# Attention rows stacked as high and low halves per head, W made already stacked, and row tiles of 64 for both products with W

## The chip, the cores and the metric

The kernel runs on one core of one Trainium2 chip. The metric is the device time in microseconds of one execution, the median of three.

## What is computed

Eight batches of eight heads, 576 positions, head dimension 64. First an attention with 32 landmarks per head (Nyström), then a mixing of positions and channels by Fourier transforms, then a feed-forward layer:

```python
q_lm = q.reshape(B, H, 32, 18, 64).mean(axis=3)      # and k_lm
A, Bm, C = sm(q, k_lm), sm(q_lm, k_lm), sm(q_lm, k)  # softmax of scaled scores
Z = Bm.T / (norm1(Bm) * norminf(Bm) + 1e-6)
for _ in range(6):
    Z = 2 * Z - Z @ Bm @ Z
x = A @ Z @ C @ v                                    # heads side by side: 576 x 512
u = x + real(fft(fft(x, axis=positions), axis=channels))
un = (u - mean(u)) / sqrt(var(u) + 1e-6)
out = u + maximum(un @ w_ch1, 0) @ w_ch2             # 512 -> 2048 -> 512
```

## The kernel before, in words

Numbers are held to more than half precision as two fp16 parts, high and low; a product of two such numbers is three matmuls (high by high, high by low, low by high), written `mm3`. W stands for Z C v, 32 x 64 per head.

**Order of work.** The program first records all operations with their reads and writes (`Order.op`), and then a planner (`Order.solve`) places them engine by engine by phase and rank, with estimated durations (`cost_of`, `mm`), buffers and PSUM banks being handed out as it goes. Operations between `together` and `apart` become one bundle on TensorE. Each engine then runs its list in that order. Attention of all batches has the higher priority, the feed-forward chunks fill in. Of the PSUM banks four are "at" (attention), two "hp", two "acc"; from chunk 5 on, two of the "at" banks are kept by the feed-forward part (`seven`, `held_banks`). SBUF buffers called "mt" (512 columns, five of them) are handed out in the order of their making.

**A batch** (`attention`): landmarks by reduction, the splits of q, and then `landmarks`, which makes the softmax of B (`nrm`), the scores of C, and six iterations on `RE`, whose columns 0 to 31 are the iterated matrix and 32 to 95 become the factor of W; a head is a block of 32 partitions, four blocks for each of two groups g of four heads. W = `RE` part times `nrm`, in two orientations: `ps` (landmarks on partitions) and `pst` (channels on partitions). After the scale `sc` (a sum over W, `pow2`), twelve splits (each a ScalarE operation and a VectorE one) move W into two kept tiles that are zero elsewhere: `Wx`, block diagonal for four heads with 256 columns, and `Wt`, two heads stacked in 128 rows.

**A's rows.** The scores of A are taken for three tiles u (two of 512 columns, a rest of 128), the softmax goes to `ae`, which is split into `hl` as all high parts and then all low parts, and transposed by DMA into `AT` (y for high and low, then four blocks of 128).

**The two products with W.** `rest()` multiplies `Wt` with the cosine and sine tables `t2`: four bundles (g, x) of six matmuls, 128 rows by 64 columns of weights, 262 moving columns, the two results in halves of one bank. `mix` runs over three row tiles nt: first the sums of CS with those results, then for each sign sg a bundle of six matmuls, `AT` as weights and `Wx` moving with 256 columns, then three additions on VectorE into the row tile `u`, which goes on to `norm` and the feed-forward chunks.

**Feed-forward.** `chunk` and, from chunk 5 on, `seven` take two row tiles (256 rows) each through `w1` and `w2`, whose preparation (`weights`, `sums_of`, `differences_of`) lies in the first part of the program.

All operations are issued through one helper, so the profile gives them all the line L1184; they are told apart by tile names: `at`, `hp`, `acc` are PSUM banks, `t` the tables.

Of the kernel before, what the change touches and what calls it, by code (L numbers as in the profile page):

```python
# [60 lines left out]
def tables():  # L61
# [8 lines left out]
    for x, fn in enumerate((np.cos, np.sin)):  # L70
        t1t[:, x] = trig(fn, REST * 2, freqs[0::2] + freqs[1::2], S)
        for r in range(4):
            h0, h1 = GROUPS[r // 2][2 * (r % 2) : 2 * (r % 2) + 2]
            cols = [*range(D * h0, D * h0 + D), *range(D * h1 + D - 1, D * h1 - 1, -1)]
            t2[:, r, :, x] = trig(fn, cols, [f or 0 for f in FREQS], DM) * np.array(there)
# [30 lines left out]
class View:  # L106
# [42 lines left out]
    def box(self):  # L149
# [5 lines left out]
        high = low + sum(step * (n - 1) for step, n in ap[1:]) + 1  # L155
# [215 lines left out]
def cost_of(engine):  # L371
# [3 lines left out]
    def cost(name, out, reads, rest):  # L375
# [19 lines left out]
class Kernel:  # L395
    def __init__(self, ctx, tc, NB, q, k, v, w1, w2, t1, t1t, t2, diag, mask, out):
# [230 lines left out]
    def attention(self, b):  # L627
# [61 lines left out]
        for u in range(3):  # L689
# [25 lines left out]
        for u in range(3):  # L715
            ae, w = aes[u], 512 if u < 2 else 128
            AT = (self.mid(512).bitcast(F16) if u < 2 else self.small(256, "AT2", F16)).rearrange("p (y t) -> p y t", y=2)
            hl = (self.row(1024, F16) if u < 2 else self.small(256, "hl2", F16)).rearrange("p (y t) -> p y t", y=2)
            self.A.copy(hl[:, 0], ae)
            self.E.tensor_tensor(hl[:, 1], ae, hl[:, 0], ALU.subtract)  # L720
            for y in range(2):
                self.turn(AT[:, y].rearrange("p (c t) -> p c t", t=P), hl[:, y])
            ATs.append(AT)
            if u == 2:
                Fs.append(hl)
                break
# [34 lines left out]
    def landmarks(self, b, loads, qbd, lm):  # L761
# [70 lines left out]
        V.tensor_scalar(nci, ci, -1.0, None, ALU.mult)  # L832
        BT = small([P, 2, 32], "BT", bufs=1)
# [62 lines left out]
        wm = small(1, "wm")  # L896
        V.tensor_reduce(wm, ps[:, 0:128], AX.X, ALU.add, apply_absolute_value=True)
        ew, rw = self.pow2(wm, 1, "wx")
# [5 lines left out]
        for o in range(2):  # L904
            rows = slice(64 * o, 64 * o + 64)
            for r in range(2):
                self.split(
                    *(Wt[rows, y, r::2, 32 * o : 32 * o + 32] for y in range(2)),
                    pst[r][rows, 0:64].rearrange("p (g m) -> p g m", g=2), sc[rows, 0:1],
                )  # L910
        for i, at in enumerate((0, 32, 160, 128)):
            rows = slice(32 * i, 32 * i + 32)
            wv = Wx[rows, :, :, at : at + 96]
            pv = ps[rows, 0:128].rearrange("p (g m o) -> p g m o", g=2, o=2)
            for o in range(2):
                self.split(*(wv[:, y, :, 64 * o : 64 * o + 32] for y in range(2)), pv[..., o if i % 2 == 0 else 1 - o], sc[rows, 0:1])

        def rest():
            WC = [self.mid().bitcast(F16)[:, 0 : 4 * NC].rearrange("p (y x t) -> p y x t", y=2, x=2) for g in range(2)]
            for g in range(2):  # L920
                for x in range(2):
                    ps = self.at()
                    self.order.claim(WC[g])
                    self.together()
                    for ya, yb in ((0, 0), (0, 1), (1, 0)):
                        for r in range(2):
                            mm(ps[64 * r : 64 * r + 64, 0:NC], Wt[:, ya, 2 * g + r, :], self.t2[:, 2 * g + r, yb, x, :],
                               yb == 0 and ya == 0, ya == 1, 0.5)
                    self.apart()
                    self.split(WC[g][:, 0, x], WC[g][:, 1, x], ps[:, 0:NC], 2.0**-15)  # L930
# [4 lines left out]
    def mix(self, b, AT, CS, WC, Wx, x2, x13):  # L935
# [3 lines left out]
        for nt in range(3):  # L939
# [18 lines left out]
            uts = []  # L958
            for sg in range(2 if nt < 2 else 1):
                ps = self.at()  # L960
                at = P * (3 - nt if sg else nt)
                pv = ps.rearrange("p (a m) -> p a m", a=8)
                if nt < 2:
                    ut = self.new("u")
                elif b2 == 0:
# [286 lines left out]
```

## Time and profile before

| | us |
|---|---|
| median of 3 runs | 1012.71 |
| lowest and highest | 1012.39, 1014.78 |
| the profiled execution | 1016.18 |
| its span, first to last instruction | 1014.40 |
| its TensorE clock, mean | 0.976 of full speed |

The profile is of one execution. The groups of instructions name what is written and read; `PE` is the matmul stream, `PEld` the loading of weights, which overlaps it. A matmul's own duration includes its way through the array, so it is the distance of two starts that says what one costs. Most rows of interest are therefore from the timeline: the start of the group that follows, less the start of this one.

### The profile page before, as it was taken

Reading aid. Unit: us, or ns where it says so; the run is one execution under the profiler, and the core shown is the slowest. Engines: PE = TensorE matmul, PEld = TensorE weight load, DVE = VectorE, ACT = ScalarE, POOL = GpSimd, SP = SyncE. Lnnn points to the kernel's source line nnn. Section 1 sums busy time; section 2 is a strip of 40 time slices with the busy share of each in tenths; the row PEclk is TensorE's granted clock in tenths of the full one; section 3 lists DMA queues with packets and bytes.
Section 4 is the critical chain, followed back from the end, with each engine's and each line's share of the span. In section 5 each row is a group of like instructions: output and inputs, shape, how many; then the busy total and the mean of one; then the engine's idle time right before and its main releaser. Section 6 shows DMA issues by size and latency. Waiting matters only on the chain.

```text
span 1014.4 us, 24771 instructions
## 1 busy us (share of the span) xinstructions
PE 948.1 (93%) x9858; PEld 751.9 (74%) x9858; DVE 778.6 (77%) x2082; ACT 488.6 (48%) x1045; POOL 191.3 (19%) x218
## 2 busy tenths in 40 slices
PE   4566998999999999999999999999999999999997
PEld 3345656666667567888888888888888788888886
DVE  6989896699897898668986888698976657575455
ACT  5989843245543443445553655355533343433332
POOL 0211020024542122122112033122211110011010
PEclk9697998999999999999999999999999999999999
DMA  9965010444422312345434533443343413344231
GB/s 342 314 252 160 24 35 12 128 117 96 175 85 62 98 54 45 89 116 173 123 94 122 168 89 104 131 150 122 104 115 90 120 48 95 94 118 126 87 100 47
DMA packets 139396, 117.28 MB, mean 116 GB/s; under 512 B 66704, under 2 KB 128144, under 8 KB 139152
## 3 DMA queue, kind: packets, MB, share of 16 engines
q1 hardware_dynamic: 139280, 115.69, 38.2%
q8 instruction: 77, 1.26, 0.5%
q14 instruction: 39, 0.32, 0.1%
HBM read 88.91 MB, written 12.58 MB: 100 GB/s over the span
## 4 chain that ended last, share of the span: by engine, by line
PE 66%; DVE 17%; ACT 9%; DMA 3%; issue 2%; SPq 1%; POOL 0%; DVEq 0%; ACTq 0%
PE hp L1184 29%; PE at L1184 20%; PE acc L1184 18%; DVE u L1184 2%; ACT w L1184 2%; ACT Wx L1184 2%; DVE Wx L1184 1%; DVE mt L1184 1%; DVE ws L1184 1%; DVE h L1184 1%; ACT ws L1184 1%; DVE row L1184 1%; DMA big<-k_dram 1%; ACT big L1184 1%; DVE lm L1184 1%
## 5 line engine op out<-in xcount | busy, mean ns | idle before, releaser
L1184 PEld LDWEIGHTS <-w 128*128 128x128 f16 (+1 forms) x3584 | 344.8, 99 | 66.5 <-DVE w L1184 12.9
L1184 PE MATMUL hp<-unT,w 128*128 128x256 f16 x3264 | 390.5, 275 | 0.1
L1184 PEld LDWEIGHTS <-h 128*128 128x128 f16 x2508 | 239.0, 98 | 66.8 <-issue 5.8
L1184 PE MATMUL acc<-w,h 128*128 128x256 f16 (+1 forms) x1260 | 205.3, 300 | 0.4 <-DVE h L1184 0.2
L1184 DVE TENSOR_TENSOR sum<-ws 128x256 f32<-128x256 f32 (+1 forms) x261 | 94.9, 410 | 96.3 <-ACT ws L1184 92.7
L1184 ACT ACTIVATE ws<-hp 128x512 f32<-128x512 f32 x104 | 62.0, 596 | 165.4 <-PE hp L1184 165.2
L1184 ACT CAST h<-sum 128x640 f16<-128x640 f32 x104 | 75.4, 725 | 64.8 <-DVE sum L1184 50.9
L1184 PE MATMUL at<-big,h 128*128 128x256 f16 x624 | 102.2, 273 | 0.0
L1184 POOL TENSOR_TENSOR sum<-ws 128x256 f32<-128x256 f32 (+1 forms) x51 | 36.2, 723 | 307.6 <-ACT ws L1184 224.6
L1184 DVE TENSOR_TENSOR h<-sum,h 128x640 f16<-128x640 f32 x83 | 68.4, 824 | 24.3 <-ACT h L1184 23.8
L1184 DVE TENSOR_REDUCE lm<-big 128x32 f32<-128x576 f32 (+1 forms) x48 | 44.7, 945 | 17.9 <-DMA big<-k_dram 16.0
L1184 PE MATMUL at<-w,h 128*128 128x256 f16 x312 | 51.1, 273 | 0.0
L1184 PE MATMUL acc<-big,h 128*128 128x256 f16 x312 | 51.1, 273 | 0.0
L1184 PEld LDWEIGHTS <-mt 128*128 128x128 f16 x432 | 39.5, 102 | 14.8 <-issue 5.7
L1184 PEld LDWEIGHTS <-big 128*128 128x128 f16 (+1 forms) x768 | 39.6, 103 | 10.5 <-issue 5.6
L1184 ACT CAST h<-ws 128x256 f16<-128x256 f32 x104 | 42.1, 405 | 2.8
L1184 DVE SCALAR_TENSOR_TENSOR u<-at,scw,row 128x128 f32<-128x128 f32 (+3 forms) x120 | 39.6, 387 | 2.6 <-PE at L1184 2.2
L1184 DVE SCALAR_TENSOR_TENSOR u<-acc,winv,u 128x512 f32<-128x512 f32 x49 | 34.8, 745 | 7.1 <-PE acc L1184 7.1
L1184 POOL TENSOR_TENSOR h<-sum,h 128x640 f16<-128x640 f32 x21 | 30.9, 1470 | 47.7 <-ACT h L1184 47.7
L1184 DVE TENSOR_TENSOR h<-ws,h 128x256 f16<-128x256 f32 x87 | 36.3, 418 | 0.0
L1184 POOL TENSOR_TENSOR ws<-ws 128x256 f32<-128x256 f32 (+1 forms) x31 | 24.2, 788 | 52.2 <-DVE ws L1184 26.3
L1184 ACT ACTIVATE big<-big 128x1168 f16<-128x1168 f32 (+1 forms) x26 | 25.4, 990 | 14.9 <-DMA big<-q_dram 14.5
(192 smaller groups left out, 1362.9 us busy)
## 6 DMA issues: line engine op xcount, KB each, us to landing
big<-sums SPq DMA_DIRECT2D x312, 128.0 KB, 2.1
w<-w_dram SPq DMA_DIRECT2D x22, 512.0 KB, 7.9
big<-v_dram SPq DMA_DIRECT2D x16, 640.0 KB, 4.7
big<-q_dram SPq DMA_DIRECT2D x16, 584.0 KB, 5.8
big<-k_dram SPq DMA_DIRECT2D x16, 576.0 KB, 5.3
out_dram<-u SPq DMA_DIRECT2D x36, 256.0 KB, 2.3
big<-w_dram SPq DMA_DIRECT2D x10, 512.0 KB, 5.4
sums<-ws SPq DMA_DIRECT2D x24, 128.0 KB, 1.7
```

The source lines that it names most:

```text
L1184: getattr(engine, name)(*map(real, args), **{k: real(x) for k, x in kw.items()})
```

## The change

Four things are done. (1) A's softmax is written as head, then high and low, then 32 landmarks, so that a transposed block holds two heads, each with its high and low part in 64 rows; the rest tile keeps its plain split in `rest` and gets one more copy. (2) W comes from products with block-diagonal copies of `nrm` (`nbd`, two elementwise operations of 256 columns), which hold the landmarks twice, so that each head's W leaves TensorE twice, one copy below the other, for the high and the low rows of A: two fp32 matmuls for `pst` and eight for `ps`, over 128 rows; two wide splits take the place of twelve, and nothing has to be zeroed. (3) Both products with W use halves of 64 rows; the product with `t2` has two bundles of 24 matmuls (tiles of 64 rows by 32 columns, a bank for each g), the mix one bundle for both signs, two matmuls of 64 columns for each head (high and low part of `Wx`; the weights hold both parts of A, so low by low is included), a bank for each half of the rows. (4) The planner's estimates are changed for small operations, and edges are added between uses of the banks. The tables `t2` change their layout with it, and the extent of a view with a negative step is computed.

The diff, with the tables and the extent of views left out:

```diff
-            return 0.07 + rate * n + 0.03 * pointers, 0.08, not psum and (full > 1 or quick) and n > 4
+            least = 0.28 if psum and pointers and out.dtype == F16 else 0.0
+            return max(least, 0.07 + rate * n + 0.055 * pointers), 0.08, not psum and (full > 1 or quick) and n > 4
...
-            return 0.09 + 0.79e-3 * n + (0.06 if pointers else 0.0) + extra, 0.1, False
+            least = 0.31 if psum and pointers and out.dtype == F16 else 0.0
+            return max(least, 0.09 + 0.79e-3 * n + (0.08 if pointers else 0.0)) + extra, 0.1, False
...
-        self.Wx = self.kept([P, 2, 2, 256], F16, "Wx")
-        self.Wt = self.kept([P, 2, 4, 64], F16, "Wt")
-        for t in (self.Wx, self.Wt):
-            self.G.memset(t, 0.0)
+        self.Wx = self.kept([P, 2, 4, 64], F16, "Wx")
+        self.Wt = self.kept([P, 2, 4, 32], F16, "Wt")
...
-            held = max(0.03, 0.003 + n / 2400 * share)
+            held = max(0.02, 0.003 + n / 2400 * share + (0.01 if share < 1.0 or 100 < n < 200 else 0.0))
...
-                    mm3(ps[rows, at + 64 * pr : at + 64 * pr + 64],
+                    mm3(ps[rows, at : at + 128].rearrange("p (h r m) -> p h r m", h=2, r=2)[:, :, pr],
...
-            hl = (self.row(1024, F16) if u < 2 else self.small(256, "hl2", F16)).rearrange("p (y t) -> p y t", y=2)
-            self.A.copy(hl[:, 0], ae)
-            self.E.tensor_tensor(hl[:, 1], ae, hl[:, 0], ALU.subtract)
-            for y in range(2):
-                self.turn(AT[:, y].rearrange("p (c t) -> p c t", t=P), hl[:, y])
+            hl = self.row(1024, F16) if u < 2 else self.small(256, "hl2", F16)
+            hy = hl.rearrange("p (h y m) -> p h y m", y=2, m=32)
+            av = ae.rearrange("p (h m) -> p h m", m=32)
+            if u == 2:
+                rest = self.small([P, 2, 128], "rest", F16, bufs=1)
+                self.A.copy(rest[:, 0], ae)
+                self.E.tensor_tensor(rest[:, 1], ae, rest[:, 0], ALU.subtract)
+                self.A.copy(hy, rest.rearrange("p y (h m) -> p h y m", m=32))
+            else:
+                self.A.copy(hy[:, :, 0], av)
+                self.E.tensor_tensor(hy[:, :, 1], av, hy[:, :, 0], ALU.subtract)
+            for x in range(0, 8 if u < 2 else 2, 4):
+                n = min(4, AT.shape[1])
+                self.turn(AT[:, x : x + n], hl[:, P * x : P * x + P * n])
...
+        nbd = self.mid(512).rearrange("p (g i m) -> p g i m", g=2, i=4)
+        for g in range(2):
+            self.E.tensor_tensor(
+                nbd[:, g].rearrange("p i (d m) -> p i d m", d=2), nrm[:, g, 0].unsqueeze(1).unsqueeze(1).broadcast_to([P, 4, 2, 32]),
+                self.mask4.unsqueeze(2).unsqueeze(3).broadcast_to([P, 4, 2, 32]), ALU.mult,
+            )
...
-        ps, pst = self.at(), [self.at(), self.at()]
+        pst = self.at()
         self.together()
         for g in range(2):
-            for i in blocks:
-                mm(ps[i, 64 * g : 64 * g + 64], nrm[i, g, 0, :], RE[i, g, 32:])
+            mm(pst[64 * g : 64 * g + 64, 0:128], RE[:, g, 32:], nbd[:, g, :, 0:32])
         self.apart()
+        self.order.ops[-1].before.update(self.used[1])
+        self.used[1] = {}
+        wm = small(1, "wm")
+        V.tensor_reduce(wm, pst[:, 0:128], AX.X, ALU.add, apply_absolute_value=True)
+        count = len(self.order.ops)
+        ew, rw = self.pow2(wm, 1, "wx")
+        total = self.order.ops[count]
+        ps = self.at()
         self.together()
         for g in range(2):
-            for i, rows in enumerate(blocks):
-                o, r = i % 2, i // 2
-                mm(pst[r][64 * o : 64 * o + 64, 32 * g : 32 * g + 32], RE[rows, g, 32:], nrm[rows, g, 0, :])
+            for i in range(4):
+                at = 64 * (2 * g + i % 2)
+                w = RE[:, g, 32:].rearrange("p (m o) -> p o m", o=2)
+                mm(ps[64 * (i // 2) : 64 * (i // 2) + 64, at : at + 64], nbd[:, g, i],
+                   w[:, ::-1] if i % 2 else w)
         self.apart()
...
+        self.order.ops[-1].before[total] = None
+        self.order.ops[-1].before.update(self.used[0])
+        self.used[0] = {}
...
-        for o in range(2):
-            rows = slice(64 * o, 64 * o + 64)
-            for r in range(2):
-                self.split(
...
-        for i, at in enumerate((0, 32, 160, 128)):
...
-            for o in range(2):
-                self.split(*(wv[:, y, :, 64 * o : 64 * o + 32] for y in range(2)), pv[..., o if i % 2 == 0 else 1 - o], sc[rows, 0:1])
+        for W, src in ((Wt, pst[:, 0:128]), (Wx, ps[:, 0:256])):
+            self.split(*(W[:, y].rearrange("p a b -> p (a b)") for y in range(2)), src, sc[:, 0:1])
...
-            for g in range(2):
-                for x in range(2):
-                    ps = self.at()
...
-                    for ya, yb in ((0, 0), (0, 1), (1, 0)):
-                        for r in range(2):
-                            mm(ps[64 * r : 64 * r + 64, 0:NC], Wt[:, ya, 2 * g + r, :], self.t2[:, 2 * g + r, yb, x, :],
...
+            for x in range(2):
+                pss = [self.at(), self.at()]
...
+                for ya, yb in ((0, 0), (0, 1), (1, 0)):
+                    for i in range(4):
+                        at = 32 * (2 * (i % 2) + i // 2)
+                        for g in range(2):
+                            rows = slice(64 * g, 64 * g + 64)
+                            mm(pss[g][at : at + 32, 0:NC], Wt[rows, ya, i], self.t2[rows, i, yb, x], yb == 0 and ya == 0, ya == 1, 0.125)
+                self.apart()
+                self.used[1][self.order.ops[-1]] = None
...
-            for sg in range(2 if nt < 2 else 1):
-                ps = self.at()
...
-                for g in range(2):
-                    mm3(pv[rows, :, 32 * g : 32 * g + 32], lambda y: AT[g][:, y, at : at + P] if nt < 2 else AT[2][:, y, 64 * g : 64 * g + 64],
-                        lambda y: Wx[:, y, g, :])
...
+            banks = [self.at(), self.at()]
+            self.order.claim(*uts)
+            self.together()
+            for sg in range(count):
+                for g in range(2):
+                    for pair in range(2):
+                        for y in range(2):
+                            for e in range(2):
+                                half = slice(64 * e, 64 * e + 64)
+                                at = 256 * sg + 64 * (pair if e == 0 else 1 - pair) + 32 * g
+                                to = banks[e][rows].rearrange("p (a m) -> p a m", m=32)[:, at // 32 : at // 32 + 5 : 4]
+                                lhs = AT[g][half, 2 * (3 - nt if sg else nt) + pair] if nt < 2 else AT[2][half, pair, 64 * g : 64 * g + 64]
+                                mm(to, lhs, Wx[half, y, 2 * g + pair], y == 0, y == 1, 0.5)
+            self.apart()
+            self.order.ops[-1].before[sums] = None
+            self.used[0][self.order.ops[-1]] = None
```

## Rows read from the trace of the kernel before

**Rows 1.** The page, busy time (us), share of the span and instructions of each engine.

```profile
PE 948.1 (93%) x9858; PEld 751.9 (74%) x9858; DVE 778.6 (77%) x2082; ACT 488.6 (48%) x1045; POOL 191.3 (19%) x218
```

**Rows 2.** The busy time of each engine by stretch: the stretch in us and its length, then for each engine busy us and (x instructions), then the granted clock of TensorE as a share of full speed, the busy share of the DMA engines and GB/s.

```profile
25.00:100.00 75.00, 44.89 (x509) 34.36 (x507) 68.36 (x180) 69.59 (x145) 14.23 (x13) 0.78 0.76 240
100.00:400.00 300.00, 288.56 (x3016) 193.56 (x3014) 253.09 (x690) 140.30 (x336) 72.96 (x80) 0.99 0.28 79
400.00:900.00 500.00, 494.04 (x5196) 419.24 (x5195) 381.65 (x1019) 226.24 (x470) 94.69 (x108) 1.00 0.38 113
```

**Rows 3.** TensorE's timeline around one pair of row tiles of the product with Wx: start us, us from the first start to the last end (matmuls overlap), engine, line, operation, out<-in with the active rows*columns, shape of the moving operand, count.

```profile
502.83 1.47 PE L1184 MATMUL at<-Wx,mt 128*128 128x256 f16 x12
504.14 0.49 PE L1184 MATMUL acc<-w,h 128*128 128x256 f16 x3
```

**Rows 4.** The same view around the last row tile of 64 rows.

```profile
838.53 0.49 PE L1184 MATMUL at<-big,h 128*128 128x256 f16 x3
838.95 0.84 PE L1184 MATMUL at<-Wx,AT 128*64 128x256 f16 x6
839.72 0.50 PE L1184 MATMUL at<-w,h 128*128 128x256 f16 x3
```

**Rows 5.** The same view around half of the product of Wt with the tables.

```profile
682.99 0.49 PE L1184 MATMUL acc<-w,h 128*128 128x256 f16 x3
683.41 0.86 PE L1184 MATMUL at<-t,Wt 128*64 128x262 f16 x12
684.21 0.50 PE L1184 MATMUL acc<-w,h 128*128 128x256 f16 x3
```

**Rows 6.** The same view around the sums of the rest tile (operands hl and t1t, 64 rows in each half), from the end of the sums of 160 columns on.

```profile
470.03 0.51 PE L1184 MATMUL at<-t,mt 128*128 128x160 f16 x5
470.47 0.58 PE L1184 MATMUL at<-t1t,hl 64*128 64x320 f16 x6
470.98 0.39 PE L1184 MATMUL hp<-unT,w 128*128 128x256 f16 x2
```

**Rows 7.** The same view around matmuls of 64 columns with weights of 128*128 (the scores of A).

```profile
517.47 0.86 PE L1184 MATMUL at<-kbd,big 128*128 128x64 f16 x24
518.16 0.41 PE L1184 MATMUL at<-ident,ml 128*128 128x128 f32 x2
```

**Rows 8.** The same view around the two products that make W.

```profile
252.84 0.81 PE L1184 MATMUL acc<-w,sum 128*128 128x512 f16 x3
253.58 0.43 PE L1184 MATMUL at<-RE,nrm 32*32 32x64 f32 x16
253.94 0.43 PE L1184 MATMUL at<-nrm,RE 32*64 32x32 f32 x16
254.31 0.39 PE L1184 MATMUL hp<-big,w 128*128 128x256 f16 x2
```

**Rows 9.** The same view around the fp32 products of 288 columns in two column tiles (scores of C).

```profile
107.02 1.19 PE L1184 MATMUL at<-big,qbd 128*64 128x288 f32 x8
108.04 0.37 PE L1184 MATMUL at<-lm,qbd 128*64 128x32 f32 x8
```

**Rows 10.** What TensorE waited for from 100 us on: us in total, times, the longest.

```profile
PE at L1184 <- DVE Wx L1184: 8.2, 6, 2.2
...
PE at L1184 <- ACT Wx L1184: 0.7, 1, 0.7
...
PE at L1184 <- DVE Wt L1184: 0.2, 1, 0.2
```

**Rows 11.** Groups of instructions, shapes kept apart: out<-in, shapes, count, then busy us and mean ns of one, then the idle time before them and who ended it. First ScalarE, then VectorE.

```profile
L1184 ACT CAST h<-ws 128x256 f16<-128x256 f32 x104 | 42.1, 405 | 2.8
...
L1184 ACT ACTIVATE Wx<-at,scw 32x64 f16<-32x64 f32 x64 | 19.6, 306 | 13.9 <-DVE Wx L1184 9.6 <-PE at L1184 3.3 <-DVE scw L1184 0.5
...
L1184 ACT ACTIVATE Wt<-at,scw 64x64 f16<-64x64 f32 x32 | 9.9, 309 | 10.9 <-PE at L1184 7.4 <-DVE scw L1184 2.9
...
L1184 ACT ACTIVATE row<-at,scw 128x262 f32<-128x262 f32 x16 | 7.8, 486 | 10.1 <-PE at L1184 10.1
...
L1184 DVE TENSOR_TENSOR mt<-mt 128x256 f32<-128x256 f32 x44 | 22.7, 534 | 2.1 <-PE at L1184 1.2 <-POOL mt L1184 0.8
...
L1184 DVE SCALAR_TENSOR_TENSOR u<-at,scw,row 128x128 f32<-128x128 f32 x64 | 18.8, 341 | 0.0
...
L1184 DVE SCALAR_TENSOR_TENSOR Wx<-at,scw,Wx 32x64 f16<-32x64 f32 x64 | 17.9, 280 | 8.0 <-ACT Wx L1184 7.0
...
L1184 DVE SCALAR_TENSOR_TENSOR row<-at,scw,row 128x262 f32<-128x262 f32 x32 | 14.2, 481 | 5.3 <-ACT row L1184 5.3
...
L1184 DVE SCALAR_TENSOR_TENSOR Wt<-at,scw,Wt 64x64 f16<-64x64 f32 x32 | 9.0, 282 | 1.9 <-ACT Wt L1184 1.3
```

**Rows 12.** The timeline of all engines from 805.2 to 808.5 us, the splits of the last batch's W and the matmul that waits for one of their banks.

```profile
805.21 0.30 ACT L1184 ACTIVATE Wx<-at,scw 32x64 f16<-32x64 f32 x1 [0.63 <-DVE Wx L1184]
...
805.55 0.28 DVE L1184 SCALAR_TENSOR_TENSOR Wx<-at,scw,Wx 32x64 f16<-32x64 f32 x1 [0.37 <-ACT Wx L1184]
805.86 0.31 ACT L1184 ACTIVATE Wx<-at,scw 32x64 f16<-32x64 f32 x1 [0.35 <-DVE Wx L1184]
...
805.93 0.30 PE L1184 MATMUL at<-nrm,RE 32*64 32x32 f32 x4
...
808.45 0.42 PE L1184 MATMUL at<-nrm,RE 32*64 32x32 f32 x12 [2.21 <-DVE Wx L1184]
```

More of the change, by code (lines that the diff above doesn't have):

```diff
@@ L71, in tables @@
         t1t[:, x] = trig(fn, REST * 2, freqs[0::2] + freqs[1::2], S)
[L72 to L75, printed above, removed]
+        for g in range(2):
+            for i, h in enumerate(GROUPS[g]):
+                cols = [*range(D * h, D * h + D)][:: -1 if i % 2 else 1]
+                t2[64 * g : 64 * g + 64, i, :, x] = trig(fn, cols, [f or 0 for f in FREQS], DM) * np.array(there)
     p = np.arange(P)
@@ L154, in box @@
         low = self.ap.offset - first * ap[0][0]
-        high = low + sum(step * (n - 1) for step, n in ap[1:]) + 1
+        high = low + sum(max(0, step) * (n - 1) for step, n in ap[1:]) + 1
+        low += sum(min(0, step) * (n - 1) for step, n in ap[1:])
         return first, first + ap[0][1], low * size, high * size
@@ L918, in rest @@
         def rest():
             WC = [self.mid().bitcast(F16)[:, 0 : 4 * NC].rearrange("p (y x t) -> p y x t", y=2, x=2) for g in range(2)]
-            for g in range(2):
-                for x in range(2):
-                    ps = self.at()
-                    self.order.claim(WC[g])
-                    self.together()
-                    for ya, yb in ((0, 0), (0, 1), (1, 0)):
-                        for r in range(2):
-                            mm(ps[64 * r : 64 * r + 64, 0:NC], Wt[:, ya, 2 * g + r, :], self.t2[:, 2 * g + r, yb, x, :],
-                               yb == 0 and ya == 0, ya == 1, 0.5)
-                    self.apart()
-                    self.split(WC[g][:, 0, x], WC[g][:, 1, x], ps[:, 0:NC], 2.0**-15)
+            for x in range(2):
+                pss = [self.at(), self.at()]
+                self.order.claim(*WC)
+                self.together()
[7 more added lines that the diff above has]
+                self.used[1][self.order.ops[-1]] = None
+                for g in range(2):
+                    self.split(WC[g][:, 0, x], WC[g][:, 1, x], pss[g][:, 0:NC], 2.0**-15)
@@ L957, in mix @@
                 V.scalar_tensor_tensor(Tt[rows, x, 0:NC], psc[rows, 0:NC], x2[rows], Qs[rows], ALU.mult, op)
-            uts = []
-            for sg in range(2 if nt < 2 else 1):
-                ps = self.at()
[L961 to L965, printed above, removed]
-                    ut = self.uR = self.new("u")
-                else:
-                    ut = self.uR
-                self.order.claim(ut)
-                self.together()
-                for g in range(2):
-                    mm3(pv[rows, :, 32 * g : 32 * g + 32], lambda y: AT[g][:, y, at : at + P] if nt < 2 else AT[2][:, y, 64 * g : 64 * g + 64],
-                        lambda y: Wx[:, y, g, :])
-                self.apart()
-                self.order.ops[-1].before[sums] = None
-                uts.append(ut)
+            count = 2 if nt < 2 else 1
@@ new lines, in mix @@
+            uts = [self.uR] if nt == 2 and b2 else [self.new("u") for sg in range(count)]
+            if nt == 2:
+                self.uR = uts[0]
+            banks = [self.at(), self.at()]
+            self.order.claim(*uts)
+            self.together()
+            for sg in range(count):
+                for g in range(2):
+                    for pair in range(2):
[6 more added lines that the diff above has]
+                                mm(to, lhs, Wx[half, y, 2 * g + pair], y == 0, y == 1, 0.5)
@@ L977, in mix @@
+            self.apart()
+            self.order.ops[-1].before[sums] = None
+            self.used[0][self.order.ops[-1]] = None
+            for sg, ut in enumerate(uts):
                 t0, t1 = Tt[rows, sg], Tt[rows, 1 - sg]
                 runs = lambda t: t.rearrange("p (x m) -> p x m", x=4)[:, :, 0:64]
-                u4, p4 = (t[rows].rearrange("p (x m) -> p x m", x=8) for t in (ut, ps))
-                V.scalar_tensor_tensor(u4[:, 0:4], p4[:, 0:4], x13[rows], runs(t0), ALU.mult, ALU.add)
+                u4 = ut[rows].rearrange("p (x m) -> p x m", x=8)
+                p4 = [t[rows, 256 * sg : 256 * sg + 256].rearrange("p (x m) -> p x m", x=4) for t in banks]
+                V.scalar_tensor_tensor(u4[:, 0:4], p4[0], x13[rows], runs(t0), ALU.mult, ALU.add)
@@ L981, in mix @@
                 V.scalar_tensor_tensor(
-                    u4[:, 4:6], p4[:, 4:6], x13[rows], t1[:, 1:129].rearrange("p (x m) -> p x m", x=2), ALU.mult, ALU.add
+                    u4[:, 4:6], p4[1][:, 0:2], x13[rows], t1[:, 1:129].rearrange("p (x m) -> p x m", x=2), ALU.mult, ALU.add
                 )
-                V.scalar_tensor_tensor(u4[:, 6:8], p4[:, 6:8], x13[rows], runs(t1)[:, 2:4], ALU.mult, ALU.add)
+                V.scalar_tensor_tensor(u4[:, 6:8], p4[1][:, 2:4], x13[rows], runs(t1)[:, 2:4], ALU.mult, ALU.add)
@@ L1156, in run @@
     def run(self):
-        self.unit, self.sums = 0, []
+        self.unit, self.sums, self.used = 0, [], [{}, {}]
         self.ntile, self.utiles, self.unT = 0, [], []
```

13 lines of the change are left out of this document (2 added, 11 removed).

## The prediction

> **What bounds the kernel now.** I began with the busy table of the page: TensorE is busy 93% of the span, VectorE 77%, ScalarE 48% [rows 1]. A share over the whole span hides stages, so next came the table of stretches [rows 2]. From 25 to 100 us ScalarE (69.6 of 75 us) and VectorE (68.4) are nearly full and TensorE is not (44.9): that is the first batch's attention together with the preparation of the weights. From 100 us on TensorE is busy 288.6 of 300, then 494.0 of 500 us, at a granted clock of 0.99 to 1.00, which is the 2.4 GHz level. So three prices count: TensorE's time for batches 1 to 7, TensorE's waits after 100 us, and ScalarE's and VectorE's work for batch 0. The reader should not add up anything else; a microsecond of ScalarE in batch 5 is worth nothing unless TensorE waits for it.
>
> The waits of TensorE after 100 us are few, and one line leads them: 8.2 us in 6 waits on VectorE's writing of Wx, 0.7 on ScalarE's, 0.2 on Wt [rows 10]. The timeline shows why. The 12 splits of W use ScalarE and VectorE in turn on one tile, some 0.65 us from one to the next (805.21 to 805.86, though one takes 0.30 and 0.28), and the matmul that needs their PSUM bank stands still for 2.21 us [rows 12].
>
> **The product of the attention rows with W.** Before, a pair of row tiles is 12 matmuls of 256 columns: 502.83 to 504.14, 1.31 us or 0.109 each, with no loss at either end [rows 3]. The last tile of 64 rows has 6: 838.95 to 839.72, and 0.09 us before it (three matmuls of 0.109 from 838.53 end their turn at 838.86), so 0.86 [rows 4]. Per batch 2 x 1.31 + 0.86 = 3.48 us.
>
> After, a pair is 32 matmuls of 64 columns, and the two halves (rows 0 to 63 and 64 to 127, into two different banks) can run at once, so 16 steps. The price of a step: 24 matmuls of 64 columns, each with its own weights of 128 x 128, took 0.69 us, 29 ns each [rows 7]; weights and columns both keep that pace. Whether halves of 64 rows run in pairs is shown by the rest-tile sums: three pairs of 320 columns took 0.51 us, where 320 columns alone are 0.133 us (three are 0.40, six one by one would be 0.80) [rows 6]. The same rows price the change into tiles and back: five matmuls of 160 columns from 470.03 should hand over at 470.37, the first tile starts at 470.47, and 0.11 is left at the end, 0.21 us in all. So a pair costs 16 x 0.029 + 0.21 = 0.68 us and the last tile 8 x 0.029 + 0.21 = 0.45. Per batch 1.81 us; saved 3.48 - 1.81 = 1.67. No row has short columns and row halves together; the lower bound of the saving is 32 single steps (0.93 + 0.21 = 1.14 per pair, 0.68 for the last), which saves 0.5. I take the upper value, since the paired rows are the same form with longer columns.
>
> **The product of W with the cosine and sine tables.** Before, 24 matmuls of 262 columns in two column tiles: a run of 12 takes 683.41 to 684.21 and 0.09 ahead of it, 0.89 us; two runs make 1.78 per batch [rows 5]. Six pairs of 0.109 are 0.655, so in, out and settling cost 0.235. After, each of two bundles has 24 matmuls in 8 tiles of 64 x 32, three rounds. With 0.12 a round, 3 x 0.12 + 0.235 = 0.59, 1.19 per batch, saved 0.6. If only the four column tiles ran together, six steps would give 0.89 again and nothing would be saved.
>
> **Making W.** Before, 32 small fp32 matmuls, 0.36 and 0.37 us with 0.10 ahead (three of 512 columns, 0.213 each, from 252.84) [rows 8], 0.83. After, 2 of 128 fp32 columns side by side and 8 of 64. Four pairs of 288 fp32 columns took 1.02 us, 0.255 a pair [rows 9], so 128 columns are 0.11 and 64 are 0.057. With 0.21 each for tiles, 0.32 and 0.44 (pairs) to 0.67 (one by one): 0.76 to 0.99. I take no change.
>
> **Sum on TensorE**: 2.27 us per batch, of which 7 batches lie where TensorE is the limit: 15.9. Bounds 4 (no row halves at once: 0.5 + 0 per batch) and 20 (one batch has its table product in four single runs).
>
> **The splits and copies.** Removed per batch on ScalarE: 8 x 0.306 + 4 x 0.309 = 3.68 us; added: two wide ones, 0.49 (that of 262 columns from PSUM) and some 0.40 for 128 columns, and one more copy of the rest tile, 0.41 (that of 256 columns): 2.4 us less. On VectorE: 8 x 0.280 + 4 x 0.282 = 3.37 removed; 0.48 and 0.34 for the splits and twice 0.53 for the block-diagonal copies of B, which GpSimd may take as well: 1.5 us less [rows 11]. The stacked order of A's halves moves no instruction: as many elements and two transposes for each big tile, one instead of two for the rest tile on SP's queue. The copies now write runs of 32 columns; the nearest rows that do so are the splits of Wx, 64 columns in 0.306 us against 262 plain ones in 0.486, which shows no penalty that I could read, so I bound it by nothing and by one more copy of 0.41 us per batch, hidden after 100 us.
> What that is worth: in batch 0, where both engines are full, 1.5 to 2.4 us; I take 2 (0 to 4). After 100 us the zigzag of 12 splits becomes one of 2, and the waits of 9.1 us lose their cause. Something late remains (the sum for the scale, its reciprocal, the two splits), so I take 6.5 away, between 3 and 9.
>
> **What is added in waits.** Every bundle of W's table product and of the mix now asks for two banks at once, where one did before, and VectorE's six additions start after both tiles' matmuls instead of three after the first. Queued behind such a matmul on TensorE is the feed-forward work of other tiles, in the order that the planner wrote; it stands only where the planner was too early. The block-diagonal tile takes one of five "mt" buffers until W is made, so the first softmax tiles may come later; in batch 0 that costs something, later nothing. New costs in the planner's tables move the whole order. I put 3 us on all of this, between 0 and 8, from the waits of 0.7 to 2.2 us that one such miss costs now [rows 10, 12]. Between 200 and 400 us VectorE may take up 1 us of TensorE's gain.
>
> Sum: -15.9 - 6.5 - 2 + 3 + 1 = -20.4. The profiled execution took 1016.2 us (span 1014.4 and 1.8 around it), so 995.8 in its own terms; the median of the runs is 3.5 lower, 1012.7, so 992.3. I say **992**. Its own range: the small ends, 4 is left to the rival below, so 13 + 3 + 0 - 8 = 8 less, to the large ends, 20 + 9 + 4 = 33 less: 980 to 1004, and with the ends not all together 983 to 1002.
>
> **Rivals.** First, **the row halves don't run at once**: each matmul then costs its 29 ns alone, and the change does not do on TensorE what it says. Then TensorE saves 0.5 us per batch, 3.5 to 4 in all, and the sum is -4 - 6.5 - 2 + 4 = -8.5, 1004 us. For it: no row with 64 columns in row halves. Against: the pairs of 320 columns [rows 6], and 16 small tiled matmuls in 0.36 us [rows 8], 22 ns each with the entry, less than the 29 of one after another. The Trainium skill, page "TensorE: Matmul & The Clock Gate", section "Wait — 56ns, not 53.3ns?", says that matmuls never start closer than about 25 ns however short; by it 80 matmuls cost 2.0 us per batch instead of 1.2, an estimate of 5 to 6 us less gain in all, near this rival. The 22 ns, entry included, speak against the rule for separate tiles.
>
> Second, and ending slower: **the pair of banks**. The code keeps two of the four "at" banks for good once the last kind of chunk starts, at about 400 us; then a bundle that needs two needs all. Batches 4 to 7 have five such new bundles each, 20 in all. If the planner places them where the last reader of a bank is late, each costs what the wait of 2.21 us shows [rows 12]. It decides when more than 11 of the 20 stand (24 us gained against 2.2 each); with 16 of 20 the time is 1012.7 - 24 + 35 = 1024. Against it: the sums over CS already ask for two banks at a time, and TensorE is still busy 494 of 500 us there [rows 2].
>
> Third, the gain is real and **eaten up elsewhere** (VectorE from 200 to 400 us, the new order, the buffer): within 3 us of 1012.7.
>
> **Chances**: forecast 0.78, halves one by one 0.10, pair of banks 0.06, eaten up 0.06. The first two are faster by over 0.3% (3 us, about what a measurement can tell from no change): faster 0.88, same 0.06, slower 0.06. The range takes in the forecast's own and the first rival: 982 to 1005.
>
> **What would show it.** In the timeline of the changed kernel, 32 matmuls on Wx should span about 0.7 us, not 1.1; the 24 with Wt about 0.5; the waits of TensorE on Wx should fall from 8.2 us to under 3; the first chunk's feed-forward work should start some 2 us sooner. A new wait on u or ml with more than 2 us, repeated from batch 4 on, would prove the prediction wrong, as would a busy TensorE with the same sum of time.

## The result and the profile after

| | before | after |
|---|---|---|
| median, us | 1012.55 | 983.04 |
| lowest and highest | 1009.38, 1014.78 | 982.05, 983.10 |
| profiled execution | 1016.18 | 983.10 |
| its span | 1014.40 | 981.30 |

The ratio is 0.971, with a 95% interval from 0.968 to 0.974: 29.5 us faster where 20.4 were forecast. The time lies 1 us inside the end of the range, 982. The two profiled executions differ by 33.1 us in span, more than the medians, because the profiled one of before was 3.6 us above its median; sums over rows below are to be held against 33.1.

The busy table of the changed kernel, beside [rows 1]:

```profile
PE 927.6 (95%) x10354; PEld 735.3 (75%) x10354; DVE 761.3 (78%) x2003; ACT 467.3 (48%) x973; POOL 202.7 (21%) x231
```

TensorE is busy 20.5 us less, and the part of the span in which it is not went from 66.3 to 53.7 us, 12.6 less. So less than two thirds of the gain is work that TensorE no longer has. The stretches, beside [rows 2] (same columns):

```profile
25.00:100.00 75.00, 49.48 (x623) 37.99 (x621) 68.18 (x171) 70.27 (x141) 16.45 (x17) 0.74 0.76 256
100.00:400.00 300.00, 295.15 (x3298) 200.89 (x3296) 253.85 (x690) 138.90 (x321) 81.91 (x93) 0.99 0.27 81
400.00:900.00 500.00, 496.76 (x5614) 422.52 (x5613) 382.76 (x997) 219.31 (x441) 97.75 (x109) 1.00 0.41 116
```

From 100 to 900 us TensorE stood idle for 4.9 + 3.2 = 8.1 us, against 11.4 + 6.0 = 17.4 before: 9.3 us less. Its waits from 100 us on, beside [rows 10]:

```profile
PE at L1204 <- DVE u L1204: 3.7, 5, 1.1
PE hp L1204 <- DVE sum L1204: 2.0, 1, 2.0
PE at L1204 <- ACT ml L1204: 1.8, 2, 0.9
PE acc L1204 <- DVE u L1204: 0.3, 1, 0.3
```

Not one wait on Wx or Wt is left (9.1 us before). The others, on additions into u, sums and evacuations into ml, add up to 7.8 us, much as the others did before (7.7). TensorE's timeline of the changed kernel at the places that answer to [rows 3, 4, 5 and 8]: the last matmuls of the weights' preparation, a pair of row tiles, a last row tile, one bundle of the table product, and the two bundles that make W (the code has two and eight fp32 matmuls there, the trace four and sixteen instructions: each fp32 matmul shows as two).

```profile
102.00 0.63 PE L1204 MATMUL acc<-w 128*128 128x128 bf16 x8
...
429.72 0.64 PE L1204 MATMUL at<-Wx,mt 64*128 64x64 f16 x32
430.29 0.39 PE L1204 MATMUL acc<-w,h 128*128 128x256 f16 x2
...
733.33 0.44 PE L1204 MATMUL at<-Wx,AT 64*64 64x64 f16 x16
733.70 0.50 PE L1204 MATMUL acc<-w,h 128*128 128x256 f16 x3
...
414.18 0.53 PE L1204 MATMUL at<-t,Wt 64*32 64x262 f16 x24
414.64 0.61 PE L1204 MATMUL hp<-unT,w 128*128 128x256 f16 x4
...
528.62 0.44 PE L1204 MATMUL at<-mt,RE 128*64 128x128 f32 x4
529.00 0.50 PE L1204 MATMUL acc<-w,h 128*128 128x256 f16 x3
...
538.76 0.74 PE L1204 MATMUL at<-RE,mt 128*64 128x64 f32 x16
539.44 0.50 PE L1204 MATMUL at<-w,h 128*128 128x256 f16 x3
```

The pair takes 429.72 to 430.29, 0.57 us, where it was 1.31; the last tile 0.37, where it was 0.77; a bundle with Wt 0.46, where a run of 12 took 0.80; each has 0.09 or 0.10 ahead of it. The two bundles of W are the exception: 0.38 and 0.68, where they were 0.36 and 0.37. The splits, beside [rows 11]:

```profile
L1204 ACT ACTIVATE Wx<-at,scw 128x256 f16<-128x256 f32 x8 | 3.8, 469 | 6.5 <-PE at L1204 6.5
...
L1204 ACT COPY hl<-rest 128x256 f16<-128x256 f16 x8 | 3.2, 402 | 1.1 <-DVE rest L1204 1.1
...
L1204 ACT ACTIVATE Wt<-at,scw 128x128 f16<-128x128 f32 x8 | 2.9, 366 | 13.7 <-DVE scw L1204 13.5
...
L1204 DVE SCALAR_TENSOR_TENSOR Wx<-at,scw,Wx 128x256 f16<-128x256 f32 x8 | 3.7, 464 | 0.0
...
L1204 DVE SCALAR_TENSOR_TENSOR Wt<-at,scw,Wt 128x128 f16<-128x128 f32 x8 | 2.7, 342 | 0.5 <-ACT Wt L1204 0.5
...
L1204 POOL TENSOR_TENSOR mt<-nrm,mask 128x256 f32<-128x256 f32 x16 | 12.3, 785 | 47.4 <-DVE nrm L1204 29.1 <-DVE sc L1204 17.4 <-POOL wp1r L1204 0.9
```

On ScalarE 0.469 + 0.366 + 0.402 = 1.24 us per batch in place of 3.68, as worked out. The block-diagonal copies were all taken by GpSimd, so VectorE lost 2.6 us instead of 1.5.

The sum of the rows, for batches 1 to 7. Mix: 2 x 0.67 + 0.46 = 1.80 us in place of 3.48, 11.8 in all. Table product: 1.10 per batch where its bundles stand apart and 0.89 where they adjoin, in place of 1.78, some 5.4. W: 0.38 + 0.68 + 0.18 for entries = 1.24 in place of 0.83, 2.9 lost. So 14.3 us of TensorE's work. The waits are 9.3. The weights' last matmuls start at 102.0 instead of 106.7 (the row of before stands here, since none above shows it), 4.7:

```profile
106.68 0.40 PE L1184 MATMUL acc<-w 128*128 128x128 bf16 x4 [0.33 <-DVE w L1184]
```

That makes 28.3 of 33.1 us. A further part is the granted clock. Three of the waits of before were over 2 us, and in two of the stretches that hold one the clock fell (columns as in [rows 2]):

```profile
150.00:175.00 25.00, 22.19 (x176) 15.93 (x175) 14.47 (x46) 8.81 (x24) 1.04 (x2) 0.86 0.10 29
800.00:825.00 25.00, 22.79 (x219) 18.00 (x218) 13.49 (x36) 11.59 (x29) 1.51 (x2) 0.93 0.22 69
```

0.14 and 0.07 of 25 us, 5.2 us of array time that was not granted. In the changed kernel the same stretches are at full speed, and one other, around a wait of 2.0 us on sum, is not:

```profile
150.00:175.00 25.00, 25.00 (x320) 18.05 (x319) 17.84 (x51) 7.63 (x17) 2.13 (x3) 1.00 0.01 2
175.00:200.00 25.00, 22.96 (x152) 15.24 (x150) 17.36 (x30) 7.06 (x12) 4.02 (x4) 0.93 0.54 149
800.00:825.00 25.00, 25.00 (x266) 21.59 (x264) 15.86 (x37) 9.59 (x18) 2.82 (x3) 1.00 0.33 96
```

1.7 us there, so 3.5 less was lost after 100 us. Together 31.8 of 33.1.

The last two terms are looser than the sum makes them look. What is exact is the split into 20.5 us less of busy and 12.6 less of idle time; of the 12.6, 9.3 lie between 100 and 900 us and 3.2 in the first 100 us, where TensorE is busy 60.3 us in place of 57.1. So the start is worth 3.2 by idle time and 4.7 by the row. And what the clock gave back after 100 us it took before: from 25 to 100 us it stands at 0.74 in place of 0.78, 3 us of 75, and its mean over the whole span is 0.975 in place of 0.976. That the 3.5 us are part of the gain is not shown.

### The profile page after: what moved, and what is told of

The parts are those of the page before. It is cut to its first block, busy times and chain, and to the rows that moved or that the text cites. A ratio compares the mean times of both kernels' runs of the same rounds, so it can differ in the third digit from the quotient of the medians.

```text
span 981.3 us, 25574 instructions
## 1 busy us (share of the span) xinstructions
PE 927.6 (95%) x10354; PEld 735.3 (75%) x10354; DVE 761.3 (78%) x2003; ACT 467.3 (48%) x973; POOL 202.7 (21%) x231
## 4 chain that ended last, share of the span: by engine, by line
PE 83%; DVE 8%; ACT 6%; issue 1%; DMA 1%; SPq 0%; POOL 0%; DVEq 0%; ACTq 0%
PE hp L1204 36%; PE at L1204 24%; PE acc L1204 23%; ACT w L1204 2%; DVE u L1204 2%; ACT ws L1204 1%; ACT big L1204 1%; ACT row L1204 1%; DVE row L1204 1%; DVE sum L1204 1%; ACT ml L1204 1%; ACT h L1204 1%; DMA big<-q_dram 1%; DVE w L1204 1%; DVE h L1204 1%
## 5 line engine op out<-in xcount | busy, mean ns | idle before, releaser
L1204 DVE TENSOR_TENSOR sum<-ws 128x256 f32<-128x256 f32 (+1 forms) x266 | 97.9, 416 | 82.0 <-ACT ws L1204 80.9
L1204 POOL TENSOR_TENSOR sum<-ws 128x256 f32<-128x256 f32 (+1 forms) x46 | 32.0, 712 | 234.0 <-ACT ws L1204 189.4
L1204 DVE TENSOR_TENSOR h<-ws,h 128x256 f16<-128x256 f32 x94 | 40.7, 433 | 0.0
L1204 PEld LDWEIGHTS <-mt 64*128 64x128 f16 (+1 forms) x752 | 28.6, 98 | 15.3 <-issue 9.7
L1204 POOL TENSOR_TENSOR r<-ve,mhalf 128x2 f32<-128x2 f32 (+1 forms) x20 | 18.0, 899 | 82.5 <-DVE ve L1204 78.0
```

The lines of the kernel that those rows point to most:

```text
L1204: getattr(engine, name)(*map(real, args), **{k: real(x) for k, x in kw.items()})
```

## The experiments

Two theories stood against each other from the first run on. A, the prediction's: TensorE's waits on Wx came from twelve splits in a zigzag and went because two are left. B: they came from the planner, which took a small split for shorter than it is (by its old formula 0.20 us on ScalarE for 64 columns from PSUM with a scale, where the trace has 0.306), and went because it was told better. In the prediction the new estimates were only a disturbance. Ratios below are to the kernel before as measured beside each run; its median went from 1012.6 to 1013.7 us between them, so a difference of 1 us from the changed kernel says nothing.

**Estimates alone.** The kernel before with the four changed lines of the planner's costs:

```diff
-            held = max(0.03, 0.003 + n / 2400 * share)
+            held = max(0.02, 0.003 + n / 2400 * share + (0.01 if share < 1.0 or 100 < n < 200 else 0.0))
...
+            least = 0.28 if psum and pointers and out.dtype == F16 else 0.0
+            return max(least, 0.07 + rate * n + 0.055 * pointers), 0.08, not psum and (full > 1 or quick) and n > 4
...
+            least = 0.31 if psum and pointers and out.dtype == F16 else 0.0
+            return max(least, 0.09 + 0.79e-3 * n + (0.08 if pointers else 0.0)) + extra, 0.1, False
```

> The kernel before with nothing but the planner's new estimates (for small splits, for tiled and short matmuls). Theory A (the waits went because twelve splits in a zigzag became two): the zigzag is still there, so the time stays near before, 1008 to 1016 us, and TensorE's waits on Wx stay above 5 us. Rival B (the waits went because the planner now knows what the splits cost): the waits on Wx fall under 2 us and the time is 1000 to 1005 us.

Measured: 1003.94 us, ratio 0.991 (0.988 to 0.994). That is B's time: 9.0 us below the kernel before, with the same operations in another order (17 of them on GpSimd in place of VectorE). Its wait on Wx, and the two stretches whose clock had fallen:

```profile
PE at L1186 <- DVE Wx L1186: 2.3, 5, 0.9
```

```profile
150.00:175.00 25.00, 24.52 (x220) 17.93 (x219) 17.55 (x54) 7.70 (x20) 1.41 (x2) 1.00 0.07 25
800.00:825.00 25.00, 24.59 (x251) 20.29 (x251) 15.89 (x41) 11.82 (x26) 2.77 (x3) 1.00 0.17 49
```

8.2 us have become 2.3, a little over the 2 that B gave, and the clock is at 1.00 in both stretches.

**The changed kernel with the old estimates** (the same lines the other way).

> The changed kernel with the planner's old estimates. Theory A: within 3 us of the changed kernel, 980 to 986 us. Rival B: the waits come back, 990 to 997 us.

Measured: 985.18 us, ratio 0.972 (0.969 to 0.975), 2.1 above the changed kernel: A's time. Its stretches from 100 to 900 us:

```profile
100.00:400.00 300.00, 293.50 (x3266) 198.69 (x3264) 252.03 (x689) 136.11 (x312) 76.31 (x87) 1.00 0.27 79
400.00:900.00 500.00, 498.32 (x5635) 422.88 (x5633) 372.96 (x982) 221.08 (x444) 105.00 (x122) 1.00 0.42 117
```

6.5 + 1.7 = 8.2 us idle, as with the new estimates. So both theories hold, each in its own kernel. Either the planner knows the price of the twelve splits, or there are no longer twelve: either removes the waits, and the two gains don't add (9.0 alone, 2.1 on top).

**The estimates taken apart.** Only the four lines for VectorE and ScalarE, and only the matmul line. The first half holds the two floors and also a higher price for every operation with a pointer operand (0.03 to 0.055 and 0.06 to 0.08), which the expectation doesn't mention.

> The kernel before with only the planner's new floors for small splits on ScalarE and VectorE (0.31 and 0.28 us). All the new estimates together took it from 1012.9 to 1003.9 us. If the waits on Wx came from the planner taking a split to be shorter than it is, this half carries it: 1002 to 1006 us, waits on Wx under 3 us. If it is the matmul estimates: 1010 to 1015 us.

> The other half: the kernel before with only the new estimates for tiled and short matmuls. By the same reason 1010 to 1015 us with waits on Wx above 5 us; if the matmul estimates carry the gain, 1002 to 1006 us.

Measured: 1006.00 us, ratio 0.993 (0.990 to 0.995), and 1016.50 us, ratio 1.004 (1.002 to 1.006). Waits of TensorE on Wx after 100 us, first with the split floors, then with the matmul line:

```profile
PE at L1186 <- DVE Wx L1186: 1.6, 3, 0.8
```

```profile
PE at L1184 <- DVE Wx L1184: 7.8, 5, 2.2
```

The half with the floors carries it; floors and pointer price were not run apart. The matmul line alone makes the kernel slower, and the halves don't add: 7.7 less and 2.8 more by themselves, 9.0 less together. My reading is that the planner had put the matmul that needs the bank where the bank would have been free if splits were as short as it believed; no run shows its plan itself.

**Twelve pieces again.** The changed kernel with W's splits cut as before. The planner finds no order for it by itself, since the next batch's products with v take the last banks and wait for a scale; they were made to wait first.

```diff
-        for W, src in ((Wt, pst[:, 0:128]), (Wx, ps[:, 0:256])):
-            self.split(*(W[:, y].rearrange("p a b -> p (a b)") for y in range(2)), src, sc[:, 0:1])
+        for o in range(2):
+            rows = slice(64 * o, 64 * o + 64)
+            for r in range(2):
+                self.split(*(Wt[rows, y, r::2] for y in range(2)), pst[rows, 0:128].rearrange("p (a m) -> p a m", a=4)[:, r::2], sc[rows, 0:1])
+        for i in range(4):
+            rows = slice(32 * i, 32 * i + 32)
+            for o in range(2):
+                self.split(*(Wx[rows, y, o::2] for y in range(2)), ps[rows, 0:256].rearrange("p (a m) -> p a m", a=4)[:, o::2], sc[rows, 0:1])
...
         V.reciprocal(ci, ci)
+        scale = self.order.ops[-1]
...
+            self.order.ops[-1].before[scale] = None
             V.tensor_scalar(RE[:, g, 32:96], ps[:, 0:64], crs[g], ci[:, g : g + 1], ALU.mult, ALU.mult)
```

> The changed kernel with W split in twelve pieces again (four for Wt, eight for Wx, across the groups as before), and one planner edge more (the products with v wait until the scale of the iteration is known), without which the planner finds no order. Theory A: the zigzag is back, 6 to 9 us of TensorE waits after 100 us and 2 to 4 us more at the start, 991 to 996 us. Rival B: the planner knows what the pieces cost and puts other work there, under 987 us.

Measured: 995.89 us, ratio 0.983 (0.980 to 0.986), 12.9 above the changed kernel. The wait is back although the planner has the new floors. The pieces of Wx are 128 columns wide here; it gives them 0.31 us on ScalarE and they take 0.36, so they are still taken for shorter than they are, but no run gave it the right price for these pieces:

```profile
PE at L1212 <- DVE Wx L1212: 7.4, 5, 2.7
```

**The control**, the additional edge without the pieces.

> The control for the run with twelve splits: the changed kernel with nothing but the additional planner edge. If the pieces made that run slow: 981 to 986 us. If the edge did: over 990 us.

Measured: 987.12 us, ratio 0.974 (0.971 to 0.976); the interval reaches that of the changed kernel, and the time lies in neither of the two ranges. The edge may cost up to 4 us, and so 8.8 to 12.9 us are the pieces'. The stretches of the two runs, first with twelve pieces, then the control:

```profile
0.00:100.00 100.00, 59.63 (x696) 41.85 (x697) 77.49 (x223) 83.43 (x174) 22.38 (x27) 0.68 0.76 249
100.00:400.00 300.00, 294.34 (x3108) 199.15 (x3106) 252.82 (x670) 145.26 (x331) 77.13 (x87) 1.00 0.29 86
400.00:900.00 500.00, 493.94 (x5732) 415.72 (x5730) 387.14 (x1045) 234.32 (x493) 124.23 (x145) 1.00 0.42 117
...
0.00:100.00 100.00, 58.29 (x724) 42.69 (x725) 83.35 (x240) 81.93 (x168) 21.41 (x27) 0.73 0.84 277
100.00:400.00 300.00, 294.21 (x3285) 201.51 (x3283) 248.73 (x667) 138.95 (x317) 86.82 (x96) 1.00 0.27 80
400.00:900.00 500.00, 497.67 (x5640) 422.31 (x5639) 376.86 (x988) 219.18 (x444) 100.83 (x116) 1.00 0.41 116
```

The two profiles are 12.6 us apart in span. From 100 to 900 us TensorE stands idle for 11.7 us against 8.1, only 3.6 more, since other waits are shorter, and the clock falls once behind the wait of 2.7 us, 1.7 us of array time. Before 100 us the clock is 0.68 against 0.73, 5 us of 100. So the waits on Wx explain less than half of what twelve pieces cost here; more lies at the start than the 2 to 4 us that theory A gave it.

**Twelve pieces in the first batch alone** (the same pieces under `if b == 0`, no edge needed).

> The changed kernel with W split in twelve pieces in the first batch alone. Theory A prices the start at 2 to 5 us of the 12.9 that twelve pieces cost in all batches: 985 to 988 us. If the start, where ScalarE and VectorE are full, bears most of it: 991 us or more. If it bears nothing: under 984.5.

Measured: 986.61 us, ratio 0.973 (0.970 to 0.976), 3.6 above the changed kernel and within theory A's range, with overlapping intervals. ScalarE and VectorE are nearly full there, and the preparation of the weights ends 7 us later than in the changed kernel:

```profile
109.27 0.39 PE L1214 MATMUL acc<-w 128*128 128x128 bf16 x4
```

Not all of those 7 us arrive at the end; that feed-forward work had been done ahead of it is my reading, not shown.

**The zigzag itself.** The kernel before with the columns of Wx and Wt ordered so that no split writes between another's columns.

```diff
-        self.Wx = self.kept([P, 2, 2, 256], F16, "Wx")
+        self.Wx = self.kept([P, 2, 8, 2, 32], F16, "Wx")
...
-                self.split(*(wv[:, y, :, 64 * o : 64 * o + 32] for y in range(2)), pv[..., o if i % 2 == 0 else 1 - o], sc[rows, 0:1])
+                self.split(*(Wx[rows, y, at // 32 + 2 * o] for y in range(2)), pv[..., o if i % 2 == 0 else 1 - o], sc[rows, 0:1])
```

> The kernel before with the columns of Wx and Wt laid out so that no split's output lies between the columns of another (twelve splits, same shapes). Theory A in its narrow form (it is the alternation of two engines on one stretch of memory that holds the bank): ScalarE runs ahead, the splits take about half as long, waits on Wx fall from 8 us to under 3, 1002 to 1008 us. If it is the number of splits alone: 1009 to 1015 us.

Measured: 1014.84 us, ratio 1.002 (1.000 to 1.003). But it did not take away what it was to take away: TensorE still waits 6.4 us on Wx after 100 us, and around the last batch's W the two engines still take turns (all engines, columns as in [rows 12]):

```profile
808.17 0.28 DVE L1183 SCALAR_TENSOR_TENSOR Wx<-at,scw,Wx 32x64 f16<-32x64 f32 x1 [0.37 <-ACT Wx L1183]
808.48 0.31 ACT L1183 ACTIVATE Wx<-at,scw 32x64 f16<-32x64 f32 x1 [0.34 <-DVE Wx L1183]
808.82 0.28 DVE L1183 SCALAR_TENSOR_TENSOR Wx<-at,scw,Wx 32x64 f16<-32x64 f32 x1 [0.37 <-ACT Wx L1183]
```

So it says nothing on the alternation; that the price lies in the alternation rather than in the number of splits stays open.

**The halves one after the other.** In the changed kernel, the loop over the halves (e) put outermost in the mix, and the loop over g ahead of that over i in the table product, with the planner told 1.0 and 0.25 for the shares.

```diff
-            for sg in range(count):
-                for g in range(2):
-                    for pair in range(2):
-                        for y in range(2):
-                            for e in range(2):
+            for e in range(2):
+                for sg in range(count):
+                    for g in range(2):
+                        for pair in range(2):
+                            for y in range(2):
```

> The changed kernel with all matmuls of the lower 64 rows first and then all of the upper 64, in the mix (bundle of 32) and in each round of W's table product; the planner is told the longer times. Theory A (the pairing of the halves is what TensorE saves): 32 matmuls take about 1.05 us instead of 0.57, the 16 of the last tile 0.6 instead of 0.37, the 24 with Wt 0.8 instead of 0.46, 1.9 us per batch and 13 to 15 in all: 995 to 999 us. Rival C (the saving is that of short columns, the halves need not alternate, or the array pairs them by itself): 982 to 986 us.

Measured: 986.74 us, ratio 0.973 (0.970 to 0.975), in neither range and much nearer to C's than to A's. The bundles, in the order table product, pair, last tile:

```profile
424.74 0.53 PE L1204 MATMUL at<-t,Wt 64*32 64x262 f16 x24
425.20 0.50 PE L1204 MATMUL acc<-w,h 128*128 128x256 f16 x3
...
432.42 1.00 PE L1204 MATMUL at<-Wx,mt 64*128 64x64 f16 x32
433.36 0.50 PE L1204 MATMUL hp<-unT,w 128*128 128x256 f16 x3
...
591.70 0.59 PE L1204 MATMUL at<-Wx,AT 64*64 64x64 f16 x16
592.22 0.61 PE L1204 MATMUL hp<-unT,w 128*128 128x256 f16 x4
```

The pair takes 0.94 us and the last tile 0.52: 0.37 and 0.15 more, 0.89 per batch and 6.2 in seven, of which 3.7 show in the time; this profile is also idle for 0.9 us less from 100 to 900 us and loses no clock there. So the pairing is real, but about half of the mix's gain is there without it: a pair moves 32 x 64 = 2048 columns in place of 12 x 256 = 3072 and goes from 1.31 to 0.94, and with pairing to 0.57. Each half writes its own bank, so half and bank take turns together, and the run doesn't tell which of the two counts. The bundle with Wt did not change (0.46): its eight tiles of a round are all different, and both orders of issue took the same time. My expectation that grouping by g would part them was wrong.

**Alternating columns** when W is made: `for i in (0, 2, 1, 3)`.

> The changed kernel with the eight fp32 matmuls that make W for the mix in the order 0, 2, 1, 3, so that the two column tiles take turns. If the two column tiles then run together: this bundle falls from 0.68 to about 0.42 us, 2 us in all, 980.5 to 982 us. If the order makes no difference to the array: 983 us.

Measured: 981.42 us, ratio 0.968 (0.966 to 0.970), 1.6 below the changed kernel with overlapping intervals. The time lies in the range of the first case, but the bundle doesn't: it falls from 0.68 only to 0.62, not to 0.42:

```profile
538.54 0.69 PE L1204 MATMUL at<-RE,mt 128*64 128x64 f32 x16
539.16 0.50 PE L1204 MATMUL at<-w,h 128*128 128x256 f16 x3
```

That is 0.4 us in seven batches, so the rest of the 1.6 is not shown to come from it. It is the fastest median of all that ran, by less than the runs can tell apart.

**A bundle for each sign.** `together` and `apart` moved inside the loop over sg.

> The changed kernel with a bundle of 16 for each sign in place of one of 32 for both, the same matmuls. If getting into row halves and back costs the 0.2 us that the rows show, 14 more such changes cost 3 us: 985 to 988 us, and each bundle of 16 takes about 0.37 us to the next start with 0.09 ahead. If it costs nothing by itself: 981 to 984 us.

Measured: 983.15 us, ratio 0.971 (0.968 to 0.974). The planner put the two bundles side by side each time, and TensorE stayed in row halves:

```profile
428.41 0.64 PE L1204 MATMUL at<-Wx,mt 64*128 64x64 f16 x32
428.98 0.50 PE L1204 MATMUL acc<-w,h 128*128 128x256 f16 x3
```

0.57 us for the 32, as in one bundle. So the run says nothing on the price of a change into halves; the 0.2 us rests on the timeline alone.

## Why the prediction was right, and where it was off

**The mix** was right as a term: 0.68 us for a pair and 0.45 for the last tile were worked out, 0.67 and 0.46 came. The choice of the paired price over the single one was the right one; the run with the halves in turn gives 0.94 for the single, and 0.10 ahead of it, where 0.93 and 0.21 for both ends was the bound.

**The table product** was right: 0.59 a bundle forecast, 0.55 came, and less where two adjoin.

**Making W** was mis-sized: no change was taken, 0.76 to 0.99 us the bounds, 1.24 came. The prediction took instructions for matmuls: the 32 of [rows 8] are 16 matmuls, and the eight of [rows 9] are four, two pairs and not four. So a pair of 288 columns took 0.51 us and not 0.255, which makes 0.23 for a pair of 128 columns and 0.11 for one of 64. With the same 0.21 for the ends that gives 0.44 and 0.66, 1.10 in sum, much nearer to the 1.24. Taking turns on the column tiles gives 0.62 in place of 0.68 for the eight. In sum TensorE's work fell by 14.3 us where 15.9 stood.

**The waits** are the step that failed, as a size. "I take 6.5 away" and "I put 3 us on all of this", with 1 more for VectorE, left 2.5 us; the rows show 9.3 us of idle time gone between 100 and 900 us. The clock behind such waits had no term at all, although [rows 2] already showed 0.99; 3.5 us less were lost after 100 us, but over the whole span it gave nothing back. The estimates of the planner stood on the wrong side of the sum: of "new costs in the planner's tables move the whole order" I expected a loss, and alone they are worth 9.0 us. That the twelve splits were the cause was half of it: with the right price for them the waits fall to 2.3 us, and with two splits they are gone at the old price too. So the wait needs both the twelve splits and a planner that takes them for shorter, as far as these runs go.

**The start** was taken at 2 us; the trace shows 4.7 by the row, 3.2 by idle time, and the run with twelve pieces in the first batch 3.6. VectorE lost 2.6 us of work per batch and not 1.5, since GpSimd took the block-diagonal copies; how much of the difference that makes is not shown.

**The rivals.** Halves not at once: no, though the single price would have cost only 0.89 us per batch, not 1.2. Matmuls of one half behind one another took 29 ns each (32 in 0.94 us, the way out included), in two halves 18 ns each. The Trainium skill ("TensorE: Matmul & The Clock Gate", section "Wait — 56ns, not 53.3ns?") says that starts never come closer than about 25 ns. So the trace agrees only for one half at a time. The 22 ns that the prediction set against this rival were counted per instruction; its 16 instructions are 8 fp32 matmuls, so they were no evidence of matmuls at that distance. The pair of banks: no; TensorE is idle for 3.2 of 500 us where only two banks are free. Eaten up elsewhere: no.

The forecast as a whole came out right in sign and in its causes, and 9 us short, above all since a term for disorder was put on where order was restored. That 983 still lies within 982 to 1005 owes something to luck: the low end was not set for a gain from the planner.

## What to carry to other kernels

A change in a planner's costs is a change like any other: find in the trace which waits end on the operations whose price is corrected, and give those waits a term with a sign. Where many small operations hold a bank that another engine waits for, either make them fewer or tell the planner what they take; doing both pays once. Before pricing a row, compare its count with the matmuls in the code: an fp32 matmul shows twice. And a wait of two microseconds on TensorE can cost the clock after it besides its own length: the thirteen profiles show ten waits of 1.99 us or more after 100 us, and behind six of them the granted clock fell to 0.50, the 1.2 GHz level, at a price of 1.7 to 3.5 us. The wait of 2.21 us at 808 us stands in two profiles, once with the fall and once without, so what decides is open.

## What the runs showed of the hardware

Matmuls in eight tiles of 64 rows by 32 columns took the same time in either order of issue (24 of 262 columns in 0.46 us). Matmuls in two row halves, each with its own bank, ran together only when they took turns (0.57 us for 32 of 64 columns against 0.94). Eight fp32 matmuls of 64 columns with 128 rows gained almost nothing from taking turns on two column tiles, 0.68 to 0.62 us.
